# First six head pairs of an attention stage turned by TensorE in float32, low parts subtracted in one piece, and the planner's order made anew

## The chip, the cores and the metric

The kernel runs on one core of one Trainium2 chip. The metric is device time in microseconds (us) of that core, from repeated runs; one further execution was profiled, and its trace gives every duration below. TensorE is called PE in the rows (PEld is its weight load), VectorE DVE, ScalarE ACT, GpSimd POOL; SP is the engine whose queue issues most DMAs.

## What is computed

Three stages, one behind the other: attention with a threshold, a feed-forward layer, and a soft mixture of experts over 32 slots.

```python
scores = (1/8) * q @ k^T                         # 4 batches, 8 heads, 576 x 576, head width 64
scores = where(scores >= max(scores) - tau, scores, -1e9)
attn   = exp(scores - max(scores)); attn /= attn.sum(-1) + 1e-9
x = concat_heads(attn @ v)                       # 2304 tokens x 512

h = x @ w_in;  x = max(0.01*h, h) @ w_out        # 512 -> 2048 -> 512

logits = x @ phi                                 # 2304 x 32
d = softmax(logits, over tokens); slot = d^T @ x # 32 x 512
out_e  = relu(slot_e @ w1_e) @ w2_e              # 8 experts, 4 slots each
y = softmax(logits, over slots) @ out
```

Inputs are float32, but `w_in` and `w_out` reach the kernel as 64-bit floats that it takes apart itself.

## The kernel before

**Tiles.** The 2304 tokens are 18 tiles of 128. Tiles 4 and 13 straddle two batches (64 tokens of each). For each tile, `attention(t)` works through 8 heads in 4 pairs. `head` forms the scores S (128 x 576) on PE with q split into a high part `qh` and a low part `ql`; DVE takes the row minimum of the negated scores into `th` (L1028), ACT takes the exponential into `ae` (L1055), DVE applies the threshold and sums the row into `z` (L1062).

**From weights to X.** The product with v needs the weights transposed. `moved(t, pr, ...)` does it by DMA, which takes 2-byte data: each head's `ae` is cast to float16 `ah` (L1203), the remainder `ae - ah` is the low part (L1213 for 512 columns and L1229 for the last 64), and one DMA transpose on SP's queue (L1243) turns the 9 blocks of 128 columns into `aT`. PE then multiplies 14 blocks of `aT` with the float16 high and low parts of v (`vx`, L1250) into the PSUM tile X: high by high, high by low, low by high. For a straddling tile each block is split into two halves of 64 rows, so a head takes 28 products. A function `turned` that transposes `ae` on PE in float32 is in the code, but the option `CT=()` uses it for no tile.

**Feed.** X is divided by the row sums, transposed by PE (L1104) and split into float16 parts `xT`. `feed(t, xT)` multiplies with `wh`, the float16 parts of `w_in` (L1283, 48 products of 512 columns a tile), ACT applies the leaky rectifier into `r` (L1295), PE transposes `r` (L1316, copies in L1322 and L1324), and products with `wq` (L1335, four column groups of 32) give the logits. `wq` is `w_out` times `phi`, formed once: 16 chunks of `w_out` are converted, transposed by PE (L778), copied, and multiplied with phi (L794: four float32 products, the chunk's transpose as the stationary operand, 32 columns of phi moving). `block` (L1467 and its neighbours) joins two tiles into the running softmax over tokens.

**v.** `load_v(b)` loads v of a batch in four tiles `vr` of 10 x 64 columns, sums their absolute values on ACT (L957), and `split_v` scales them (L973), casts the high part (L983) and subtracts the low part (L988).

**Order.** Nothing here runs in the order of the code. Every operation is handed to a planner (`Plan`) with a priority, a planned duration and, where two engines can do it, alternatives. `schedule` simulates the five engines and the DMA queues with these planned durations, and the order that comes out is what each engine's queue holds. Each engine then works through its own queue in that order, and waits on semaphores where an operand or a buffer isn't ready. `O` holds the options: buffer counts (`VR` is the number of `vr` tiles), priorities, and planned costs. PSUM has 2 score tiles, 1 X tile and 3 tiles `h` that all other PE results share.

**Tail.** After the last tile, `w_out` (4 MB, from a copy `scr` in device memory), `w1` and `w2` (33 MB together) are loaded into whatever buffers are free (`CH`: `wh`, `kx`, `vr`, `vx`, `r`, ...), multiplied, and the result is stored.

## Time and profile before

| | |
|---|---|
| median of 3 runs | 682.22 us (680.89 to 683.32) |
| profiled execution, its own time | 679.31 us |
| its span, first to last instruction | 677.5 us |
| PE busy | 566.5 us (84%) |
| DVE / ACT / POOL busy | 454.3 / 440.2 / 289.9 us |
| mean granted clock of PE | 0.956 |
| DMA packets | 126.37 MB, mean 187 GB/s |

PE's matmul rows overlap each other, since matmuls are pipelined, so the busy time of one row says less than the distance between two rows. In the chain of work that ended last, rows of one kind are merged, and a row's length there is that distance. A granted clock of 1.00 is the 2.4 GHz level; a stretch whose mean is lower ran part of the time at 1.2 GHz.

### The profile page before, as it was taken

What the parts mean: (1) busy time and instruction counts of PE and PEld (TensorE: products, weight loads), DVE (VectorE), ACT (ScalarE), POOL (GpSimd) and SP (SyncE); (2) the same over time, 40 slices, a digit from 0 to 9 for tenths busy, and PEclk for the clock granted to TensorE, in tenths of its full rate; (3) what the DMA queues carried; (4) which work ended last, traced back from release to release, by engine and by line L of the source; (5) the groups of instructions that cost most, each with busy time, mean ns of one, the idle gap of its engine ahead of it and who ended that gap; (6) DMA issues with size and microseconds to landing.
All of it is one profiled execution on the core that took longest, in us unless ns stands there. A gap on an engine that the chain in (4) does not pass through costs nothing.

```text
span 677.5 us, 15209 instructions
## 1 busy us (share of the span) xinstructions
PE 566.5 (84%) x5640; PEld 380.8 (56%) x5640; DVE 454.3 (67%) x1112; ACT 440.2 (65%) x825; POOL 289.9 (43%) x339
## 2 busy tenths in 40 slices
PE   0101766998899999899999999979999999789995
PEld 0000655867567776665676776757667555333553
DVE  6989869786589789788798888767888300110023
ACT  7999768775467877688977787757777344320022
POOL 3565537351244755577854566646445100000000
PEclk9999978697999999999999999989999999879997
DMA  8961799894976789868986777687679702999996
GB/s 303 320 218 60 201 204 231 235 201 156 154 139 142 160 155 155 124 118 182 174 161 119 145 138 142 131 162 150 109 110 213 181 17 93 358 314 351 349 351 235
DMA packets 224073, 126.37 MB, mean 187 GB/s; under 512 B 175872, under 2 KB 196864, under 8 KB 224000
## 3 DMA queue, kind: packets, MB, share of 16 engines
q1 hardware_dynamic: 221264, 120.43, 75.0%
q10 hardware_dynamic: 2736, 4.98, 2.7%
q8 instruction: 44, 0.72, 0.5%
q14 instruction: 29, 0.24, 0.1%
HBM read 73.99 MB, written 8.91 MB: 122 GB/s over the span
## 4 chain that ended last, share of the span: by engine, by line
PE 62%; DMA 12%; DVE 5%; ACT 4%; issue 2%; POOL 2%; SPq 0%; DVEq 0%; POOLq 0%; ACTq 0%
PE h L1283 21%; DMA aT<-ah 12%; PE S L1017 10%; PE X L1250 8%; PE S L1601 5%; PE h L1316 4%; PE X L1672 3%; PE h L1467 2%; PE h L1335 2%; PE h L794 2%; DVE ae L1028 1%; DVE ae L1062 1%; PE h L778 1%; PE h L1558 1%; POOL kx L931 1%
## 5 line engine op out<-in xcount | busy, mean ns | idle before, releaser
L1283 PE MATMUL h<-wh,xT 128*128 128x512 f16 x864 | 213.8, 381 | 0.3 <-ACT c L1363 0.3
L1213 POOL TENSOR_TENSOR ah<-ae,ah 128x512 f16<-128x512 f32 x103 | 121.8, 1184 | 94.6 <-ACT ah L1203 48.5
L1028 DVE TENSOR_SCALAR_CACHE_REDUCE ae<-S,c 128x576 f32<-128x576 f32 x144 | 115.5, 811 | 36.4 <-PE S L1017 26.5
L1055 ACT ACTIVATE ae<-ae,th 128x576 f32<-128x576 f32 x144 | 109.3, 769 | 21.2 <-DVE ae L1028 20.4
L1062 DVE SCALAR_TENSOR_TENSOR ae<-S,th,ae 128x576 f32<-128x576 f32 x144 | 114.9, 810 | 9.2 <-ACT ae L1055 7.9
L1283 PEld LDWEIGHTS <-xT 128*128 128x128 f16 x864 | 76.8, 99 | 69.5 <-issue 2.4
L1017 PE MATMUL S<-kx,qh 128*128 128x288 f32 x320 | 108.7, 357 | 8.4 <-DVE ae L1062 4.8
L1250 PE MATMUL X<-vx,aT 128*128 128x64 f16 (+1 forms) x2240 | 91.3, 197 | 17.5 <-DMA aT<-ah 17.3
L1250 PEld LDWEIGHTS <-aT 128*128 128x128 f16 (+1 forms) x2240 | 80.0, 103 | 39.6 <-DMA aT<-ah 25.7
L1017 PE MATMUL S<-kx,ql 128*128 128x288 f32 x320 | 92.3, 305 | 10.1 <-DVE ql L893 10.1
L1203 ACT ACTIVATE ah<-ae 128x576 f16<-128x576 f32 x124 | 83.6, 677 | 21.3 <-DMA aT<-ah 11.5
L1229 POOL TENSOR_TENSOR ah<-ae,ah 128x64 f16<-128x64 f32 x127 | 53.4, 422 | 62.1 <-ACT ah L1203 52.9
L1017 PEld LDWEIGHTS S<-kx,qh 128*128 128x128 f32 x320 | 61.8, 193 | 21.1 <-issue 10.2
L1017 PEld LDWEIGHTS S<-kx,ql 128*128 128x128 f32 x320 | 62.0, 194 | 11.7 <-DVE ql L893 10.4
L1295 ACT ACTIVATE r<-h 128x512 f32<-128x512 f32 x72 | 42.5, 590 | 25.8 <-PE h L1283 25.6
L1322 ACT ACTIVATE rT<-h 128x512 f32<-128x512 f32 x57 | 33.7, 594 | 29.0 <-PE h L1316 28.8
L893 POOL TENSOR_TENSOR ql<-qr,qh 128x512 fp32r<-128x512 f32 x30 | 39.2, 1306 | 22.6 <-ACT qh L884 21.9
L931 POOL TENSOR_TENSOR kx<-kr,kx 64x576 fp32r<-64x576 f32 x26 | 38.6, 1486 | 21.3 <-ACT kx L924 16.8
L1316 PE MATMUL h<-c,r 128*128 128x128 f32 x288 | 45.4, 283 | 0.8 <-ACT r L1295 0.7
L1316 PEld LDWEIGHTS h<-c,r 128*128 128x128 f32 x288 | 34.6, 145 | 8.5 <-issue 2.1
L495 PE MATMUL h<-c,tmp 128*1 128x128 f32 x16 | 4.3, 364 | 41.3 <-DVE tmp L562 38.0
L1213 DVE TENSOR_TENSOR ah<-ae,ah 128x512 f16<-128x512 f32 x41 | 32.5, 794 | 7.4 <-ACT ah L1203 6.9
(286 smaller groups left out, 842.4 us busy)
## 6 DMA issues: line engine op xcount, KB each, us to landing
qr<-in_q SPq DMA_DIRECT2D x33, 256.0 KB, 3.1
wh<-in_w SPq DMA_DIRECT2D x32, 256.0 KB, 5.6
kx<-in_w SPq DMA_DIRECT2D x22, 256.0 KB, 5.7
vr<-in_v SPq DMA_DIRECT2D x16, 320.0 KB, 3.2
rT<-in_w_out SPq DMA_DIRECT2D x20, 256.0 KB, 3.7
kr<-in_k SPq DMA_DIRECT2D x16, 288.0 KB, 3.0
r<-in_w SPq DMA_DIRECT2D x18, 256.0 KB, 5.1
ae<-in_w_in SPq DMA_DIRECT2D x8, 512.0 KB, 5.3
```

Source lines behind the costliest of these rows:

```text
L931: f = lambda eng, kx=kx, h=h, l=l: lambda: eng.tensor_tensor(out=kx.ap[l], in0=kr.ap[h], in1=f32(kx.ap[h]), op=ALU.subtract)
L1017: pe.matmul(out=ps.ap[:rows, n, :HALF], lhsT=l.ap[:, hd % 4, :rows], rhs=kt.ap[:, n * HALF : (n + 1) * HALF], start=(j == 0), stop=(j == 1 ...
L1028: lambda: dve.tensor_scalar(out=ev(), in0=ps.ap[:, :, :HALF], scalar1=nt.ap[:, 0:1], scalar2=None, op0=ALU.subtract, op1=ALU.min, accum_ou ...
L1055: lambda: act.activation(out=ae.ap[:, hd % 2], in_=ae.ap[:, hd % 2], func=AF.Exp, bias=th.ap[:, 0:1], scale=-1.0),
L1062: lambda: dve.scalar_tensor_tensor(out=ev(), in0=ps.ap[:, :, :HALF], scalar=th.ap[:, 0:1], in1=ev(), op0=ALU.is_le, op1=ALU.mult, accum_ou ...
L1203: ("act", t_act(S) + 100, (lambda i: lambda: act.activation(out=ah.ap[:, i, i * S : i * S + S], in_=ae.ap[:, i], func=AF.Copy))(i)),
L1213: f = lambda eng: lambda: eng.tensor_tensor(out=w0(ah.ap), in0=src(ae.ap), in1=hi(ah.ap), op=ALU.subtract)
L1229: f = lambda eng, i=i, lo1=lo1: lambda: eng.tensor_tensor(out=lo1(ah.ap), in0=ae.ap[:, i, (1 - i) * LC : (1 - i) * LC + D], in1=ah.ap[:, i ...
L1250: pe.matmul(out=X.ap[r0:r1, (2 * pr + i) * D : (2 * pr + i + 1) * D], lhsT=aT.ap[:, 8 - c if i else c, r0:r1], rhs=vtiles[b, pr].ap[:, wv, ...
L1283: pe.matmul(out=hp.ap, lhsT=xT.ap[:, wx * 4 + k], rhs=wh[k][j].ap[:, ww], start=(n == 0), stop=(n == 11),)
L1295: (lambda j, hp: lambda: act.activation(out=r[j].ap, in_=hp.ap, func=AF.Prelu, alpha=0.01))(j, hp),
L1316: pe.transpose(tp.ap[:, c], r[j].ap[:, c * P : (c + 1) * P], ident.ap)
```

## The change

Six things change.

1. **Turned pairs.** The option `CN={0: 4, 1: 2}` sends all four pairs of tile 0 and the last two pairs of tile 1 through `turned`. It no longer scales `ae` first, it writes the transposes (L1177) into three buffers taken from the ring `r`, and its ten float32 products (L1198) now have the transposed weights as the stationary operand and v (64 columns) as the moving one, with X in the same layout as in `moved`.
2. **Low parts in one piece.** The subtraction of the low part runs over 576 columns at once (L1229 in the new file). That shifts the low columns by 64, so v is also stored shifted by 64 rows: `vr` grows from 10 to 18 x 64 columns, `vx` from 20 to 28. `VR` goes from 5 to 4.
3. **Tail of v.** The last 64 rows of v for turned pairs come as a tile of their own (`vz`, in an `xT` buffer).
4. **w_out times phi on column groups.** Phi (32 columns) is the stationary operand now, the chunk's transpose moves (L794, four groups of 32 rows). A copy `us` and one product with `e4` (L812) add the four groups and turn the result.
5. **Straddling tiles.** The two 64-row halves of a block now follow each other directly, block by block.
6. **Planned costs.** A DMA transpose is planned at 185 instead of 112 ns a block, scores at 560 instead of 520, so the whole order is made anew. X is normalised in one way for all tiles.

```diff
-        KR=2, VR=5, ET=1, RAW=1, CP=(3,), CT=(), PM=(), PR=1, AHN=2,
+        KR=2, VR=4, ET=1, RAW=1, CN={0: 4, 1: 2}, PM=(), PR=1, AHN=2,
...
-        op = pl.add(prio, one("sp", 112.0 * blocks, fn), r, w, after)
-        op.hold = (max(1225.0, 398.0 + 112.0 * blocks), 1300.0)
+        op = pl.add(prio, one("sp", O["BT"] * blocks, fn), r, w, after)
+        op.hold = (max(1225.0, 398.0 + O["BT"] * blocks), 1300.0)
...
+        up, us = tmp([P, P], F32, "h"), tmp([P, P], F32, "lts")
+
+        def f(wt=wt, up=up):
+            for k in range(4):
+                pe.matmul(
+                    out=up.ap[32 * k : 32 * k + 32], lhsT=phi.ap[:, k], rhs=wt.ap[:, k],
+                    start=True, stop=True, skip_group_check=True,
+                )
...
-                pe.matmul(out=wpp.ap, lhsT=wt.ap[:, k], rhs=phi.ap[:, k], start=(k == 0), stop=(k == 3))
...
+            (lambda us, wpp: lambda: pe.matmul(
+                out=wpp.ap, lhsT=us.ap, rhs=e4.ap, start=True, stop=True))(us, wpp),
...
-    turns = lambda t: O["CP"] if t in O["CT"] else ()
+    turns = lambda t: range(4 - O["CN"].get(t, 0), 4)
+
+    VC = 18
...
-                ("act", t_act(10 * D) + 90, lambda: act.activation(
+                ("act", t_act(VC * D) + 90, lambda: act.activation(
                     out=vr.ap, in_=vr.ap, func=AF.Copy, scale=sv.ap[:, 0:1])),
...
-        pe_op(prio, 520 * len(todo), f, r=[qh, ql] + kts, w=[ps])
+        pe_op(prio, O["TS"] * len(todo), f, r=[qh, ql] + kts, w=[ps])
...
         def f():
-            for r0, r1, b in regs:
-                v = vflat[b, pr].ap.rearrange("p (c d) -> p c d", d=D)
+            for i in range(2):
                 for c in range(5):
-                    for i in range(2):
+                    for r0, r1, b in regs:
+                        v = vflat[b, pr].ap.rearrange("p (c d) -> p c d", d=D)
                         pe.matmul(
-                            out=X.ap[64 * i : 64 * i + 64, pr * P + r0 : pr * P + r1],
-                            lhsT=v[:, 4 * i + c if c < 4 else 8 + i],
-                            rhs=eT.ap[:, 5 * i + c if c < 4 else 4, r0:r1],
-                            start=(pr == 0 and c == 0 and r0 == 0), stop=(c == 4),
+                            out=X.ap[r0:r1, (2 * pr + i) * D : (2 * pr + i + 1) * D],
+                            lhsT=(eTs[i].ap[:, c] if c < 4 else eTs[2].ap[:, 0])[:, r0:r1],
+                            rhs=v[:, 4 * i + c] if c < 4 else vtail[b].ap[:, pr, i],
+                            start=(pr == 0 and i == 0 and c == 0), stop=(c == 4),
                             skip_group_check=True,
                         )
...
+                return lambda: eng.tensor_tensor(
+                    out=ah.ap[:, i, (1 - i) * S : (2 - i) * S], in0=ae.ap[:, i],
+                    in1=ah.ap[:, i, i * S : i * S + S], op=ALU.subtract,
+                )
...
-                for r0, r1, b in regs:
-                    for n, (c, wv, cv) in enumerate(todo):
+                for n, (c, cv) in enumerate(todo[i]):
+                    for r0, r1, b in regs:
```

What the planner makes of it is seen in three places. The first is PE's queue where tile 0's first products with v stand. S are score products, w and h under L778 and L794 are a chunk of `w_out`, c_189 and c_252 are phi, c_75 is the identity. Before, the first product with X stands behind the scores of five heads and two chunks:

```order
L1017 MATMUL S<-kx,ql 128x288
L778 MATMUL h<-c_75,w 128x128 x4
L495 MATMUL h<-c_75,tmp 1x128
L794 MATMUL h<-c_189,w 128x32 x4
L519 MATMUL h<-tmp,c_84 128x1
L1017 MATMUL S<-kx,qh 128x288
L1017 MATMUL S<-kx,ql 128x288
L1017 MATMUL S<-kx,qh 128x288
L1017 MATMUL S<-kx,ql 128x288
L1250 LDWEIGHTS aT
L1250 MATMUL X<-vx,aT 128x64
```

The same place after the change (L1060 are the scores, r is the buffer that holds the transposed weights, xT the tail of v):

```order
L1060 MATMUL S<-kx,qh 128x288
L1060 MATMUL S<-kx,ql 128x288
L1177 MATMUL h<-c_75,ae 128x128 x5
L778 MATMUL h<-c_75,w 128x128 x4
L1198 MATMUL X<-vr,r 128x64 x4
L1198 MATMUL X<-xT,r 128x64
L1198 MATMUL X<-vr,r 128x64 x4
L1198 MATMUL X<-xT,r 128x64
L794 MATMUL h<-w,c_252 32x128 x4
L1060 MATMUL S<-kx,qh 128x288
L1060 MATMUL S<-kx,ql 128x288
```

The transposes and products of a pair stand between the scores of the next heads, with no DMA between them.

The second place is PE's queue at the first feed product (L1283 before, L1288 after). Before, it follows the eleventh head's products with v, behind the scores of 17 heads:

```order
L1250 LDWEIGHTS aT
L1250 MATMUL X<-vx,aT 128x64
L1283 LDWEIGHTS xT
L1283 MATMUL h<-wh,xT 128x512
L1283 LDWEIGHTS xT
```

After, it stands behind the scores of 11 heads; x_1070 is tile 0's normalised X, and L812 is the new small product of the `w_out` chunk:

```order
L778 MATMUL h<-c_75,w 128x128 x4
L794 MATMUL h<-w,c_252 32x128 x4
L1151 MATMUL h<-c_75,x_1070 128x128 x4
L812 MATMUL h<-c_86,lts 128x32
L778 MATMUL h<-c_75,w 128x128 x4
L1060 MATMUL S<-kx,qh 128x288
L1060 MATMUL S<-kx,ql 128x288
L1060 MATMUL S<-kx,qh 128x288
L1060 MATMUL S<-kx,ql 128x288
L794 MATMUL h<-w,c_252 32x128 x4
L1288 LDWEIGHTS xT
L1288 MATMUL h<-wh,xT 128x512
```

The feed of tile 0 has moved up by the scores of six heads, and one more `w_out` chunk (ten instead of nine) has come ahead of it.

The third place is SP's queue while `w_out` is loaded (rT and raw are its buffers, scr its copy in device memory). Before, transposes stand between the loads:

```order
L591 DMA rT<-in_w_out 128x512 x2
L876 DMA qr<-in_q 128x512
L769 DMA scr<-w 128x512
L1243 DMA_TRANSPOSE aT<-ah 128x9x128
L591 DMA rT<-in_w_out 128x512 x2
L1243 DMA_TRANSPOSE aT<-ah 128x9x128
L769 DMA scr<-w 128x512
L1243 DMA_TRANSPOSE aT<-ah 128x9x128 x2
L769 DMA scr<-w 128x512
L591 DMA rT<-in_w_out 128x512
```

After:

```order
L591 DMA rT<-in_w_out 128x512 x2
L896 DMA qr<-in_q 128x512
L769 DMA scr<-w 128x512
L591 DMA rT<-in_w_out 128x512 x3
L980 DMA vr<-in_v 128x1152
L769 DMA scr<-w 128x512
L896 DMA qr<-in_q 128x512
L591 DMA rT<-in_w_out 128x512
L591 DMA raw<-in_w_out 128x512
L769 DMA scr<-w 128x512
```

The first transpose on SP's queue now stands behind all but two of the loads of `w_out` in that queue.

## Rows read from the trace of the kernel before

**Rows 1.** Windows: stretch, length, busy PE, PEld, DVE, ACT, POOL, clock, DMA, GB/s.

```profile
51.00:68.00 17.00, 1.74 (x5) 0.87 (x5) 16.63 (x36) 16.47 (x35) 8.60 (x8) 1.00 0.19 58
68.00:85.00 17.00, 13.32 (x69) 11.24 (x69) 14.61 (x36) 12.36 (x27) 9.07 (x10) 0.90 0.77 202
85.00:102.00 17.00, 11.20 (x119) 10.09 (x118) 11.54 (x35) 12.09 (x26) 5.84 (x7) 0.80 1.09 208
102.00:136.00 34.00, 27.34 (x230) 23.52 (x231) 28.97 (x68) 26.55 (x57) 17.66 (x21) 0.75 0.95 232
136.00:170.00 34.00, 30.35 (x266) 23.58 (x264) 25.96 (x60) 22.19 (x46) 10.80 (x13) 0.90 0.71 181
170.00:204.00 34.00, 30.80 (x349) 20.43 (x348) 25.03 (x58) 17.94 (x34) 12.55 (x15) 1.00 0.83 145
204.00:240.00 36.00, 36.00 (x446) 26.72 (x443) 30.82 (x68) 29.88 (x54) 23.14 (x27) 1.00 0.78 150
...
540.00:560.00 20.00, 20.00 (x163) 11.53 (x161) 1.13 (x5) 8.62 (x21) 0.50 (x1) 1.00 0.10 34
...
580.00:620.00 40.00, 33.49 (x186) 12.33 (x185) 5.13 (x14) 8.36 (x18) 0.35 (x1) 0.83 1.01 348
```

**Rows 2.** Timeline of PE: first scores, first feed products, scores of head 28.

```profile
69.07 0.61 PE L1017 MATMUL S<-kx,ql 128*128 128x288 f32 x1 [10.11 <-DVE ql L893]
...
128.47 1.95 PE L1283 MATMUL h<-wh,xT 128*128 128x512 f16 x6
...
164.88 0.38 PE L1017 MATMUL S<-kx,qh 128*128 128x288 f32 x1
```

**Rows 3.** Chain that ended last, 110 to 170 and 400 to 430 us: start, length.

```profile
118.91 1.91 PE h L794 x8
123.54 1.52 PE X L1250 x28
132.48 0.81 PE h L794 x8
...
401.14 0.41 PE X L1250 x14
401.55 1.29 PE h L1283 x6
403.90 0.44 PE h L1316 x4
406.04 1.01 PE h L1335 x32
408.31 0.14 PE h L1352 x2
419.38 0.90 PE X L1250 x28
```

**Rows 4.** Groups: line, engine, operation, count, busy us, mean ns, idle before.

```profile
L1213 POOL TENSOR_TENSOR ah<-ae,ah 128x512 f16<-128x512 f32 x103 | 121.8, 1184 | 94.6 <-ACT ah L1203 48.5 <-issue 22.6 <-DVE ah L1205 8.2
L1229 POOL TENSOR_TENSOR ah<-ae,ah 128x64 f16<-128x64 f32 x127 | 53.4, 422 | 62.1 <-ACT ah L1203 52.9 <-DVE ah L1205 5.6 <-ACT c L799 1.8
L1213 DVE TENSOR_TENSOR ah<-ae,ah 128x512 f16<-128x512 f32 x41 | 32.5, 794 | 7.4 <-ACT ah L1203 6.9
L973 ACT ACTIVATE vr<-vr,c 128x640 f32<-128x640 f32 x15 | 11.9, 816 | 0.4 <-DVE c L530 0.4
L983 ACT ACTIVATE vx<-vr 128x640 f16<-128x640 f32 x15 | 10.9, 725 | 1.4 <-PE X L1250 1.4
```

**Rows 5.** Waits of PE between 420 and 540 us: total, times, longest.

```profile
PE X L1250 <- DMA aT<-ah: 6.1, 7, 3.2
```

**Rows 6.** Timeline of ACT: the last of five passes over the next batch's v.

```profile
67.65 0.74 ACT L957 ACTIVATE xT<-vr 128x640 bf16<-128x640 f32 x1
```

**Rows 7.** Loads issued on ACT's queue, by line 591: count, ns min/median/max.

```profile
L591 ACTq DMA_DIRECT2D rT<-in_w_out x6: 334/337/434, 94.5 to 142.0; - x6
```

**Rows 8.** Waits of SP's queue between 540 and 600 us.

```profile
SPq L1589 <- PE h L1283: 31.0, 10, 15.8
```

More of the change, by code (lines that the diff above doesn't have):

```diff
@@ L406, in psum_buf @@
         return pl.buf(("h",), shape, F32, "misc")
-    pl.early.update(("T", "xp", "misc", "gT"))
+    pl.early.update(("T", "xp", "misc", "gT", "eT"))
     pl.cap["h", "h"] = 2
@@ L789, in emit @@
         )
-        wpp = tmp([P, NS], F32, "h")
-        def f(wt=wt, wpp=wpp):
-            for k in range(4):
-                pe.matmul(out=wpp.ap, lhsT=wt.ap[:, k], rhs=phi.ap[:, k], start=(k == 0), stop=(k == 3))
-        pe_op(PQ, 850, f, r=[wt, phi], w=[wpp])
+        up, us = tmp([P, P], F32, "h"), tmp([P, P], F32, "lts")
[5 more added lines that the diff above has]
+                )
+        pe_op(PQ, 330, f, r=[wt, phi], w=[up, us])
+        add_alt(
+            PQ,
+            [
+                ("act", 210, (lambda up, us: lambda: act.activation(
+                    out=us.ap, in_=up.ap, func=AF.Copy))(up, us)),
+                ("dve", 220, (lambda up, us: lambda: dve.tensor_copy(out=us.ap, in_=up.ap))(up, us)),
+            ],
+            r=[up], w=[us],
+        )
+        wpp = tmp([P, NS], F32, "h")
+        pe_op(
+            PQ, 130,
+            (lambda us, wpp: lambda: pe.matmul(
+                out=wpp.ap, lhsT=us.ap, rhs=e4.ap, start=True, stop=True))(us, wpp),
+            r=[us, e4], w=[wpp],
+        )
         act_op(
@@ new lines, in attention @@
+        dve_op(
+            p, P2(100),
+            lambda: dve.scalar_tensor_tensor(
+                out=z1.ap, in0=z.ap, scalar=1e-9, in1=zfr.ap, op0=ALU.add, op1=ALU.mult),
+            r=[z, zfr], w=[z1],
+        )
+        dve_op(p, 200, lambda: dve.reciprocal(out=rz.ap, in_=z1.ap), r=[z1], w=[rz])
+        x32 = pl.buf("x32", [P, DM])
+        dve_op(
+            p, 74 + 1.19 * DM,
+            lambda: dve.tensor_tensor(
+                out=x32.ap.rearrange("p (h d) -> p h d", d=D), in0=X.ap.rearrange("p (h d) -> p h d", d=D),
+                in1=rz.ap.unsqueeze(2).to_broadcast([P, H, D]), op=ALU.mult,
+            ),
+            r=[X, rz], w=[x32],
+        )
@@ L1122, in recip, with f @@
+        xp = pl.buf(("h",), [P, 4, P], F32, "xp")
+        def f():
+            for k in range(4):
+                pe.transpose(xp.ap[:, k], x32.ap[:, k * P : (k + 1) * P], ident.ap)
+        pe_op(p, 440, f, r=[x32, ident], w=[xp, xT])
+        act_op(
+            p, 602, lambda: act.activation(out=xT.ap[:, :4], in_=xp.ap, func=AF.Copy), r=[xp], w=[(xT, 0)]
         )
         dve_op(
-            p, 153 + 6 * (h1 - h0),
-            lambda: dve.reciprocal(out=rz.ap[:, : h1 - h0], in_=z1.ap[:, : h1 - h0]), r=[z1], w=[rz],
-        )
@@ L1258, in moved @@
             pe_op(
-                p + 0.22, 29 * 14 * len(regs), f, r=[aT] + [vtiles[b, pr] for _, _, b in regs], w=[X],
+                p + 0.22, 29 * 14 + 60 * len(regs), f, r=[aT] + [vtiles[b, pr] for _, _, b in regs], w=[X],
             )
@@ L1743, in host @@
     ka = ka.reshape(B, 4, P, S)
-    vf = v[:, :, :512].reshape(B, 4, 2, 4, P, D).transpose(0, 1, 4, 2, 3, 5).reshape(B, 4, P, 8, D)
-    vl = v[:, :, 512:].reshape(B, 4, 2, D, D).transpose(0, 1, 3, 2, 4)
-    va = np.concatenate([vf, np.concatenate([vl, vl], axis=2)], axis=3)
+    va = np.zeros((B, 4, P, 20, D), np.float32)
+    for i in range(2):
+        x = v[:, i::2]
+        cols = lambda c, r0, r1, k0: va[:, :, r0:r1, c].__setitem__(
+            slice(None), x[:, :, k0 : k0 + r1 - r0])
+        for c in range(4):
+            cols(4 * i + c, 0, P, c * P)
+        if i:
+            rest = ((9, (448, 512)), (14, (512, 0)), (15, (64, 128)), (16, (192, 256)), (17, (320, 384)))
+        else:
+            rest = ((8, (512, 0)), (10, (64, 128)), (11, (192, 256)), (12, (320, 384)), (13, (448, 512)))
+        for c, (k0, k1) in rest:
+            cols(c, 0, 64, k0)
+            cols(c, 64, P, k1)
+        cols(18 + i, 64 * i, 64 * i + 64, 512)
     def bits(w):
```

182 lines of the change are left out of this document (71 added, 111 removed).

## The prediction

> **What bounds the kernel now.** I read the windows first [rows 1]. Until 68 us TensorE has almost nothing to do (1.74 of the last 17 us) while ACT is busy 16.47 and DVE 16.63 of 17: they convert `w_in`. The first scores start at 69 us [rows 2]. From 204 us on TensorE is busy without a gap (36.00 of 36 us, clock 1.00), and it stays close to that until attention is over; from 540 to 560 us it still works off feed products while DVE has 1.13 us of work and the DMA engines are 10% busy. Then loads take over (348 GB/s from 580 us). So there are three limits: elementwise engines up to 69 us, TensorE from about 204 us to the end of the feed, and the weight loads of the tail, which wait for TensorE: SP's queue stands 31.0 us behind the last feed products that free `wh` [rows 8]. What ends the feed earlier therefore moves the whole tail.
>
> Between 68 and 204 us neither limit holds. TensorE is busy 13.32 + 11.20 + 27.34 + 30.35 + 30.80 = 113 of 136 us, so 23 us are idle, and the granted clock is 0.90, 0.80, 0.75, 0.90 and 1.00 in the five windows, which takes another 1.7 + 3.4 + 8.5 + 3.4 = 17 us of full-speed time [rows 1]. These 40 us are what an order can win. DVE is the busiest other engine there (106 of 136 us), and feed products, which would fill TensorE, do not start before 128.5 us [rows 2].
>
> **The change part by part.** Work of TensorE, from the distances in the chain [rows 3]:
>
> - *Turned pairs.* Removed: twelve heads of 14 float16 products, 0.41 us a head, 4.9 us. Added: 6 x 9 transposes. L1316 is the same operation, four in 0.44, so 5.9 us. Added: 6 x 10 float32 products with a 128-wide stationary operand and 64 columns moving, which the trace does not have. The nearest row is L794 (same stationary shape, 32 columns): four products (eight records) in 0.81 us, so 0.20 each and 12.2 us. The row shows that the load of the stationary side sets the distance, since 32 columns alone can't take 0.2 us where 128 columns of a transpose take 0.11; so I take 0.20 for 64 columns too. The lower bound is a transpose's 0.11 (6.6 us), the upper one L794 at the low clock, 1.91 us for four, 0.48 each (28.7 us).
> - *w_out on column groups.* L794 at 0.81 becomes four products like those of L1335 (16 in 1.01 us, 0.25 for four) and one like L1352 (0.14): 0.42 saved, 6.7 us over 16 chunks at the full clock.
> - Sum: -4.9 + 5.9 + 12.2 - 6.7 = 6.5 us more work at the full clock. At the low clock (0.76 for a head from the pair at 123.54, 0.48 a product, twice the transposes, w_out 1.91 to about 0.85) it is -9.1 + 11.9 + 28.7 - 17 = about 14 us.
> - *Straddling tiles.* A head takes 28 products in 0.90 us, an ordinary one 14 in 0.41 [rows 3]. In the new order neighbours write different halves of X. L1335, whose neighbours write different column groups, still takes 1.01 us for 32 records, 0.032 each; 28 records at this distance are 0.88 us, so 16 heads gain 0.3 us, nothing. The Trainium skill weighs this otherwise: "TensorE: Matmul & The Clock Gate", Part 3, says that products on different column groups run at the same time, a few ns apart. By that rule, as an estimate, a straddling head would take half of its 0.90 and the two tiles would give 7 us; the record distance of L1335 speaks against the full effect.
> - *Low parts.* POOL's 1184 and 422 ns [rows 4] become one of about 1184 plus 64 columns. The slope between the two rows is 762 ns for 448 columns, so about 1290: 0.3 us less a head. POOL and DVE are off the path in the saturated stage, so it shortens only the way from scores to `aT`.
> - *v.* Scale and cast of a `vr` tile (816 and 725 ns at 640 columns [rows 4]) grow by 1.8 at most, 1.2 us a pair, 4.9 us for batch 0, on ACT, which is full before 69 us. Against that, before the change five passes over the next batch's v stand on ACT ahead of 69 us (the last at 67.65, 0.74 and a read of the sum each [rows 6]), about 4.5 us; with four `vr` tiles, all kept by the turned pairs, they move behind tile 1. Net zero. Batch 0 brings 1.6 MB more through DMA, 4.6 us at the 348 GB/s that the tail reaches; the last window before 68 us has room (0.19 [rows 1]), but these loads stand ahead of the last of `w_in`. I take +2 us for the start, bounds 0 and +5.
> - *Loads on ACT's queue.* The order moves 26 loads from SP to ACT for the rest of the run. One costs 0.34 us [rows 7], 9 us in all over 400 us in which ACT has slack (29.88 of 36 us at the fullest); nothing, unless one waits for its buffer at the head of ACT's queue, behind which the exponentials stand.
> - *Fewer vr tiles.* One tail load less can be fetched early: 256 KB, +0.7 us.
>
> **What the order gains** is read at one point. The scores of head 28 start at 164.88 us now [rows 2]. In the order, what DVE and ACT have ahead of head 28 is alike in both versions: all of `w_in`, all 16 chunks of `w_out`, 27 first and 26 second passes. DVE loses four casts and one of four low subtractions (0.8 us each [rows 4]) and gets six copies of transposed weights and eight of `us`; ACT loses nine casts and gets twelve copies. These cancel within 3 us. So head 28 should come at the same time, 165 us, plus the 2 us of the start. But TensorE has then issued more: 81 instead of 48 feed products (33 x 0.215 = 7.1), products with v of 22 instead of 16 heads (6 x 0.41 = 2.5), 24 instead of 16 transposes of `r` (0.9), 16 instead of none of L1335 (1.0), 8 instead of 4 transposes of x (0.4), and the last `w_out` product and one L1352 (0.9). That is 12.8 us less to do from there on, the 6.5 us of extra work already behind. From 165 us TensorE is nearly full in both, so this goes to the end.
>
> It needs about 19 us more work of TensorE in the same 96 us. At the clock of these windows the work of before (about 57 us at full speed, by the distances above) fills 68; 76 us would fill 91. With the gaps filled the clock should be higher: the stretch from 204 us, without gaps, shows 1.00 [rows 1]. I charge 2 us for gaps that stay.
>
> **Later waits.** Between 420 and 540 us TensorE waits 6.1 us for transposes [rows 5]. They are now planned at 185 ns a block, and the order puts slightly more of TensorE's work between a head's scores and its products with v (in the last 24 heads 11.8 instead of 10.6 us at the distances of [rows 3]). I take 2 of the 6.1 us, bounds 0 and 6.
>
> **Sum:** -12.8 + 2 (start) + 2 (gaps) - 2 (waits) + 0.7 (tail) = -10.1 us. The profiled execution took 679.3 us by its own clock, 1.8 more than its span, so 669.2; it lies 2.9 us under the median of the three runs, so the median should be 672.
>
> **Rivals.**
>
> - *A: forecast*, 672 us. Its own range is 663 to 679: start 0 to 5, gaps 0 to 6, waits 0 to 6, products at 0.11 (-5) or a little over 0.2.
> - *B: nothing is won*, 682 us. The 20 us of idle time between 68 and 170 us come from waits for DVE and ACT in a queue that is worked through in order; if each new transpose waits for its exponential as the transposes by DMA did, head 28 slips by what TensorE has gained. For it: DVE's share there. Against it: the waits are at score and chunk rows, and the new work stands between them.
> - *C: slower*, 690 us. The low clock stays: the float32 products cost 0.48 us and stand in TensorE's queue ahead of the next scores, so that attention itself is held. Work then fills 91 us at the old mean clock, and with the old 20 us of idle time head 28 comes 15 us later, which is 2.5 us more than the gain; extra work at the low clock instead of the full one adds another 7, for 10 in all, less the waits. It decides if the granted clock from 85 to 136 us stays at 0.80 or less.
> - *D: more is won*, 660 us: the gaps close fully and the clock is 1.00 from 100 us on, so that more than the 12.8 us is ahead at head 28, and the later waits go.
> - *E: straddling halves overlap*: if the halves of a block run side by side, 16 heads of 0.90 us [rows 3] take half, 7 us on top of A, 665 us. For it is L1335, whose neighbours write different column groups: 16 float32 products of 128 columns in 1.01 us are too fast for one after another (a transpose of 128 columns takes 0.11, a float32 product two records). Against it: 0.032 a record may already be the floor. (This is the rule of the page named above.)
>
> Chances: A 0.45, B 0.16, C 0.15, D 0.12, E 0.12. About 0.3%, 2 us, is what a measurement of this kernel can tell from no change. Faster by more than that: A, D, E and a little of B, less A's upper edge, 0.69; the same 0.11; slower 0.20. The range for 8 in 10 takes in D and E, and B with part of C: 657 to 688 us.
>
> **What the profile after would show.** Right: first feed products at about 115 us instead of 128.5; head 28 at 165 to 169 us with 81 feed products before it; granted clock above 0.85 from 102 to 136 us; ten turned products of a pair in about 2 us; the last feed products 10 us earlier and a tail of the old length. Wrong: first scores later than 74 us (the v loads or the longer passes cost more), turned products at 0.4 us and a clock that stays low (C), waits of TensorE for exponentials at the new transposes (B), or a new wait for `aT` behind tile 1, where the order now leaves 10 instead of 20 us between scores and products of tiles 2 and 3.

## The result and the profile after

The changed kernel takes 657.78 us (median of 4 runs, 653.94 to 660.11), beside 681.56 us for the kernel before (4 runs, 680.29 to 683.32). The ratio is 0.9644, 95% interval 0.9588 to 0.9699: faster, by 23.8 us where 10 were forecast. Runs on another chip gave 654.77 us (6 runs) beside 676.02, ratio 0.9674 (0.9622 to 0.9726). A time here and below is the median of all runs of a kernel, and a ratio counts only the runs within 1.5% of its fastest. The profiled execution took 656.39 us against 679.31, its span is 654.6 against 677.5 us, the mean granted clock 0.982 against 0.956.

The windows of the changed kernel answer to [rows 1]; columns as there:

```profile
68.00:85.00 17.00, 13.13 (x92) 11.12 (x92) 14.78 (x33) 11.23 (x28) 4.41 (x3) 1.00 0.69 200
85.00:102.00 17.00, 14.54 (x133) 12.52 (x134) 14.42 (x37) 14.86 (x41) 1.28 (x1) 1.00 0.83 286
102.00:136.00 34.00, 28.99 (x275) 20.69 (x274) 28.16 (x66) 26.90 (x63) 6.63 (x5) 1.00 0.78 185
136.00:170.00 34.00, 32.53 (x328) 24.64 (x327) 27.39 (x68) 25.12 (x50) 13.95 (x11) 1.00 0.80 198
170.00:204.00 34.00, 33.92 (x387) 23.44 (x386) 30.36 (x79) 29.63 (x48) 19.55 (x16) 1.00 0.80 167
204.00:240.00 36.00, 36.00 (x478) 24.91 (x476) 30.77 (x79) 27.93 (x53) 17.47 (x17) 1.00 0.78 170
```

From 68 to 204 us TensorE is busy 123.11 of 136 us, 10.1 more than before, and the granted clock is at the 2.4 GHz level in every window. The line to look at twice is 170 to 204: 33.92 us of TensorE where before had 30.80, and ACT at 29.63 where before had 17.94. I had called that stretch nearly full in both.

The timeline of TensorE answers to [rows 2]: first scores, the ten turned products of a pair, first feed products, the scores of head 28 and of head 29, the last feed products.

```profile
68.65 0.61 PE L1060 MATMUL S<-kx,ql 128*128 128x288 f32 x1 [1.50 <-DVE ql L913]
...
79.53 1.00 PE L1198 MATMUL X<-vr,r 128*128 128x64 f32 x8
80.37 0.39 PE L1198 MATMUL X<-xT,r 128*128 128x64 f32 x2
80.60 1.06 PE L1198 MATMUL X<-vr,r 128*128 128x64 f32 x8
81.49 0.39 PE L1198 MATMUL X<-xT,r 128*128 128x64 f32 x2
...
111.81 0.82 PE L1288 MATMUL h<-wh,xT 128*128 128x512 f16 x3
...
166.37 0.37 PE L1060 MATMUL S<-kx,qh 128*128 128x288 f32 x1
...
169.71 0.38 PE L1060 MATMUL S<-kx,qh 128*128 128x288 f32 x1
...
558.16 1.03 PE L1288 MATMUL h<-wh,xT 128*128 128x512 f16 x4
```

The turned products of a pair take 2.3 us (79.53 to 81.81, twenty records, 0.11 each), the first feed products come 16.7 us earlier than in [rows 2], head 28 only 1.5 us later. What I had not looked at is the next head. In the kernel before, the timeline of TensorE from head 28's last score on reads:

```profile
165.35 0.29 PE L1017 MATMUL S<-kx,ql 128*128 128x288 f32 x1
...
167.20 0.57 PE L1250 MATMUL X<-vx,aT 128*128 128x64 f16 x14
167.70 1.08 PE L1335 MATMUL h<-rT,c 128*32 128x128 f32 x32
168.71 0.99 PE L1250 MATMUL X<-vx,aT 128*128 128x64 f16 x28
...
175.29 0.58 PE L1250 MATMUL X<-vx,aT 128*128 128x64 f16 x14 [2.78 <-DMA aT<-ah]
...
180.69 0.58 PE L1250 MATMUL X<-vx,aT 128*128 128x64 f16 x14
...
182.11 0.38 PE L1017 MATMUL S<-kx,qh 128*128 128x288 f32 x1
```

There the order puts the products with v of seven heads (98 products) between head 28 and head 29, and TensorE's queue is worked through in order: no scores for 17 us. SP's queue of the kernel before shows why the last of these products came late, and the window what that cost the other engines:

```profile
154.38 0.33 SPq L876 DMA_DIRECT2D qr<-in_q  x1
156.47 0.33 SPq L769 DMA_DIRECT2D scr<-w  x1
157.62 0.33 SPq L1527 DMA_DIRECT2D raw<-scr  x1
158.69 5.71 SPq L769 DMA_DIRECT2D scr<-w  x2
164.50 2.79 SPq L1527 DMA_DIRECT2D w<-scr  x4
167.34 0.42 SPq L876 DMA_DIRECT2D qr<-in_q  x1
167.81 15.31 SPq L1243 DMA_TRANSPOSE aT<-ah  x7
```

```profile
160.00:182.00 22.00, 18.95 (x214) 13.95 (x214) 10.31 (x24) 8.51 (x18) 2.12 (x3) 0.92 0.79 164
```

Seven transposes stand back to back, 2.19 us each; the old plan counted 1.41 us for one. DVE and ACT, which live on scores, have 10.31 and 8.51 us of work in 22. The same window of the changed kernel:

```profile
160.00:182.00 22.00, 21.82 (x260) 16.10 (x258) 18.08 (x47) 18.33 (x34) 14.88 (x13) 1.00 0.83 149
```

At head 29 the changed kernel is 12.4 us ahead (169.71 against 182.11), and its order has 12 feed products and 4 transposes of `r` more behind it by then (12 x 0.215 + 0.4 = 3 us), with as many heads multiplied with v: 15 us of the 22.9. At head 28, 11.3 us of them were there already (the 12.8 us of work that the prediction counts, less the 1.5 us by which that head came later), so the place itself adds some 4 us. A second part lies in the straddling tiles. In the chain of the changed kernel a head of tile 13, 28 products in [rows 3] as well, reads:

```profile
406.47 0.56 PE X L1256 x28
411.26 0.56 PE X L1256 x28
```

0.56 us instead of 0.90, over 16 heads 5.4 us. In the single records, the two halves of a block start 0.003 us apart and the next block 0.032 us later, so that 28 products start within 0.44 us; in the kernel before neighbours stand 0.032 us apart, but where the halves change, and it takes 0.78 us. The 0.12 us from the last start to the next operation are the same in both. The last feed products start 21.9 us earlier than before (558.16 against 580.01), and what follows them is 1.0 us shorter.

### The profile page after: what moved, and what is told of

Same layout as the page of the kernel before. It is cut to its first block, busy times and chain, and to the rows that moved or that the text cites. A ratio compares the mean times of both kernels' runs of the same rounds, so it can differ in the third digit from the quotient of the medians.

```text
span 654.6 us, 15007 instructions
## 1 busy us (share of the span) xinstructions
PE 555.0 (85%) x5678; PEld 370.0 (57%) x5678; DVE 452.7 (69%) x1112; ACT 447.1 (68%) x823; POOL 249.4 (38%) x208
## 5 line engine op out<-in xcount | busy, mean ns | idle before, releaser
L1288 PE MATMUL h<-wh,xT 128*128 128x512 f16 x864 | 215.3, 381 | 1.0 <-DVE xT L1159 0.9
L1229 POOL TENSOR_TENSOR ah<-ae,ah 128x576 f16<-128x576 f32 x104 | 135.3, 1308 | 151.5 <-ACT ah L1218 101.0
L1060 PE MATMUL S<-kx,qh 128*128 128x288 f32 x320 | 107.9, 354 | 13.6 <-ACT qh L904 13.3
L1288 PEld LDWEIGHTS <-xT 128*128 128x128 f16 x864 | 76.8, 99 | 68.4 <-issue 1.5
L1060 PE MATMUL S<-kx,ql 128*128 128x288 f32 x320 | 90.3, 298 | 1.5 <-DVE ql L913 1.5
L1256 PE MATMUL X<-vx,aT 128*128 128x64 f16 (+1 forms) x2072 | 75.7, 194 | 13.3 <-DMA aT<-ah 13.1
L1256 PEld LDWEIGHTS <-aT 128*128 128x128 f16 (+1 forms) x2072 | 65.9, 101 | 33.9 <-DMA aT<-ah 17.1
L1218 ACT ACTIVATE ah<-ae 128x576 f16<-128x576 f32 x108 | 72.7, 678 | 15.0 <-DVE ae L1105 8.6
L1060 PEld LDWEIGHTS S<-kx,qh 128*128 128x128 f32 x320 | 60.0, 187 | 28.3 <-POOL kx L951 13.8
L1060 PEld LDWEIGHTS S<-kx,ql 128*128 128x128 f32 x320 | 60.1, 188 | 3.1 <-DVE ql L913 1.8
L1327 ACT ACTIVATE rT<-h 128x512 f32<-128x512 f32 x51 | 30.3, 595 | 26.1 <-PE h L1321 25.7
L951 POOL TENSOR_TENSOR kx<-kr,kx 64x576 fp32r<-64x576 f32 x21 | 31.1, 1482 | 20.2 <-DVE kx L946 10.0
L1363 DVE TENSOR_REDUCE sm<-h 128x1 f32<-128x32 f32 x18 | 3.4, 189 | 36.1 <-PE h L1357 35.9
L1229 DVE TENSOR_TENSOR ah<-ae,ah 128x576 f16<-128x576 f32 x28 | 22.3, 798 | 5.2 <-ACT ah L1218 5.0
```

What stands on the lines that cost most here:

```text
L1060: pe.matmul(out=ps.ap[:rows, n, :HALF], lhsT=l.ap[:, hd % 4, :rows], rhs=kt.ap[:, n * HALF : (n + 1) * HALF], start=(j == 0), stop=(j == 1 ...
L1218: ("act", t_act(S) + 100, (lambda i: lambda: act.activation(out=ah.ap[:, i, i * S : i * S + S], in_=ae.ap[:, i], func=AF.Copy))(i)),
L1229: return lambda: eng.tensor_tensor(out=ah.ap[:, i, (1 - i) * S : (2 - i) * S], in0=ae.ap[:, i], in1=ah.ap[:, i, i * S : i * S + S], op=ALU ...
L1256: pe.matmul(out=X.ap[r0:r1, (2 * pr + i) * D : (2 * pr + i + 1) * D], lhsT=aT.ap[:, c, r0:r1], rhs=vtiles[b, pr].ap[:, cv], start=(pr == 0 ...
L1288: pe.matmul(out=hp.ap, lhsT=xT.ap[:, wx * 4 + k], rhs=wh[k][j].ap[:, ww], start=(n == 0), stop=(n == 11),)
```

## The experiments

The theories, as they stood at the start: **Q**, the transposes by DMA stand in SP's queue behind the traffic of `w_out`, and turned pairs go round it; **K**, the gain is the clock, raised by the new product of `w_out` and phi; **P**, the planned costs carry it; **O**, neighbouring products on different halves of X overlap. The expectations use these letters. Unless the text says that the order is unchanged, the planner made a new one. Ratios are to the kernel before on the same chip, with 95% intervals.

### One part undone in the changed kernel

**No turned pairs.**

```diff
-CN={0: 4, 1: 2}
+CN={}
```

> The changed kernel without turned pairs: all pairs go through DMA transposes, all else as changed, the order planned anew. Theory Q (the transposes by DMA stand in SP's queue behind the stores and loads of w_out, and the turned pairs go round that queue): 8 to 12 us are lost, 666 to 670 us; the first feed product comes after 122 us, and TensorE again waits for aT and idles between 136 and 204 us. Rival K (the gain is the clock, raised by the new form of the product of w_out and phi): 658 to 661 us, and the granted clock from 68 to 204 us stays at 1.00.

662.34 us, ratio 0.9756 (0.9678 to 0.9835), so 5 to 8 us lost, by the two ratios of the changed kernel, with intervals that still overlap. The first feed products start at 130.91 us. The granted clock from 102 to 136 us is 0.74 and TensorE is busy 25.00 of 34 us there. K falls: the new product was in, and the clock was low all the same. Q's signs are there, its size of 8 to 12 us is not quite reached; the cause is taken up below.

**The old product of w_out and phi.**

```diff
-                pe.matmul(out=up.ap[32 * k : 32 * k + 32], lhsT=phi.ap[:, k], rhs=wt.ap[:, k], ...)
+                pe.matmul(out=wpp.ap, lhsT=wt.ap[:, k], rhs=phi.ap[:, k], start=(k == 0), stop=(k == 3))
```

> The changed kernel with the old product of w_out and phi (128-wide stationary operand, 32 columns moving), the order planned anew. Theory Q: only the longer product counts, 0.4 us a chunk at the full clock, and some of it in gaps: 660 to 666 us; the granted clock from 85 to 170 us stays above 0.93. Rival K: the clock falls back to 0.75 to 0.90 from 68 to 170 us, and 12 us or more are lost: 670 us or longer.

662.09 us, ratio 0.9707 (0.9615 to 0.9800): 2 to 4 us by the middle values, inside the intervals. The clock is 1.00, 1.00, 0.85 and 1.00 in the four windows from 68 to 170 us. K falls here too.

**The old planned costs.**

```diff
-TS=560, BT=185.0
+TS=520, BT=112.0
```

> The changed kernel planned with the old costs (112 ns a block for a DMA transpose, 520 for scores). Theory Q: the operations carry the gain and not the planned costs: 656 to 662 us. Rival P (the planned costs carry it, since the order then leaves the transposes by DMA their true time): 666 us or longer, with TensorE's waits for aT doubled from 204 us on.

672.13 us, ratio 0.9868 (0.9819 to 0.9918): 13 to 15 us lost, more than by any other part. P's size, though TensorE's waits for `aT` from 170 to 540 us are 9.9 us here and 9.5 in the changed kernel, not doubled: the loss is not in that row. Much of it lies earlier. From 102 to 136 us the clock is 0.77 here, and head 29 starts 5.7 us later than in the changed kernel, with 72 instead of 90 feed products behind it (18 x 0.215 = 3.9 us); between the two profiled executions there are 15.0 us. The timeline of TensorE at heads 28 and 29:

```profile
172.58 0.38 PE L1060 MATMUL S<-kx,qh 128*128 128x288 f32 x1
...
175.38 0.48 PE L1060 MATMUL S<-kx,qh 128*128 128x288 f32 x1
```

The place where the kernel before issued no scores for 17 us is not in this order, though it was made with the old costs.

**A cost moved by 4 ns**, to see what a new order alone does.

```diff
-TS=560
+TS=556
```

> The changed kernel with one planned cost moved by 4 ns (scores at 556 instead of 560), so that the order is made anew and nothing else differs. If an order made anew moves the time by itself only little, 656 to 660 us, and differences of 4 us and more between re-planned kernels can be read as those of their edits. If the order is a lottery, it comes 4 us or more away from 657.8 us, and single re-planned kernels say little.

657.97 us, ratio 0.9692 (0.9618 to 0.9766): the same as the changed kernel within the intervals.

**The changed kernel again, the old sequence in straddling tiles, and the low part in two pieces.** The last two keep the order as it is.

> The changed kernel once more, on the chip of the next runs, for their comparison: 656 to 660 us.

```diff
-                for n, (c, cv) in enumerate(todo[i]):
-                    for r0, r1, b in regs:
+                for r0, r1, b in regs:
+                    for n, (c, cv) in enumerate(todo[i]):
```

> The changed kernel, its order unchanged, with the products of a straddling tile in the old sequence (all of one half, then all of the other). Theory O (neighbouring products that write different halves of X overlap): 28 products take 0.90 us instead of 0.56, 16 heads, 5.4 us longer than the changed kernel, 662 to 664 us. Rival (the distance was shorter for another reason, such as the clock or better placed operands): no more than 1 us longer.

```diff
-                return lambda: eng.tensor_tensor(
-                    out=ah.ap[:, i, (1 - i) * S : (2 - i) * S], in0=ae.ap[:, i], ...)
+                    for c0, c1 in ((0, S - D), (S - D, S)):
+                        eng.tensor_tensor(
+                            out=ah.ap[:, i, (1 - i) * S + c0 : (1 - i) * S + c1], in0=ae.ap[:, i, c0:c1], ...)
```

> The changed kernel, its order unchanged, with the low part subtracted in two instructions again (512 and 64 columns). If the shorter way from scores to transpose carries part of the later stretch's gain, 0.3 us a head shows as more waits of TensorE for aT: 3 to 6 us longer than the changed kernel. If POOL and DVE are off the path there: within 1.5 us of it.

The changed kernel: 654.77 us, 0.9674, a little under the range expected. Old sequence: 661.05 us, 0.9749 (0.9693 to 0.9804), the chain's rows for the same heads at 0.90 us again:

```profile
408.24 0.90 PE X L1256 x28
413.36 0.90 PE X L1256 x28
```

With the order kept, the sequence alone decides between 0.56 and 0.90 us, as O says. The time, 5 to 6 us by the middle values, agrees with 16 x 0.34 = 5.4, with intervals that still overlap. A part is paid back in waits here too: TensorE waits for `aT` 6.2 us from 170 to 540 us with the old sequence, 9.5 and 7.2 in the two profiled executions of the changed kernel. Low part in two pieces: 663.51 us, 0.9802 (0.9751 to 0.9853), 8.7 us longer, more than the 3 to 6 expected. TensorE's waits from 170 to 540 us are, in this order,

```profile
PE X L1260 <- DMA aT<-ah: 13.9, 8, 3.8
```

where the changed kernel has

```profile
PE X L1256 <- DMA aT<-ah: 9.5, 6, 2.2
```

So 0.3 us on the way to each transpose is not free: 4.4 us come back as waits of TensorE alone (6.7 against the second execution of the changed kernel, which has 7.2).

### One part alone in the kernel before

**The straddling sequence, order unchanged.**

```diff
-                for r0, r1, b in regs:
-                    for n, (c, wv, cv) in enumerate(todo):
+                for n, (c, wv, cv) in enumerate(todo):
+                    for r0, r1, b in regs:
```

> The kernel before, its order unchanged, with the two halves of each block as neighbours (two loops exchanged, nothing else). Theory O: 28 products in 0.56 instead of 0.90 us, 16 heads: 5.4 us faster than before, 675 to 677 us, ratio 0.990 to 0.994. Rival (nothing overlaps, or the time is lost again in waits for aT): 681 to 682 us, ratio 0.997 or more.

677.34 us, ratio 1.0006 (0.9976 to 1.0036): nothing. The products do take 0.56 us, but the waits in its trace from 170 to 540 us, and those of the kernel before, are:

```profile
PE X L1250 <- DMA aT<-ah: 17.6, 17, 4.0
```

```profile
PE X L1250 <- DMA aT<-ah: 13.3, 15, 3.2
```

4.3 of the 5.4 us that TensorE saves it waits longer for the transposes. These are single executions; waits of one order differed by 2.3 us between two of them (above).

**SP's queue without the traffic of w_out, order otherwise unchanged.** The copy of `w_out` is left out: its stores are gone, and the loads that read it come later, from other data.

```diff
-                (lambda c, w: lambda dq: dq.dma_start(out=scr[c], in_=w.ap))(c, w),
+                lambda dq: None,
...
-            WO, t_dma(P * DM * 4), (lambda c, wo: lambda dq: dq.dma_start(out=wo.ap, in_=scr[c]))(c, wo),
+            WO, t_dma(P * DM * 4), late_load(c, wo),
```

> The kernel before without the 16 stores of w_out's copy on SP's queue, and with the loads of that copy behind attention (from other data of the same size); all other rows in their old order. It leaves out the copy of w_out. Theory Q (before, SP's queue of transposes stands behind stores that wait for w_out's conversion): the transposes that stood still from 148 to 168 us come earlier, and 5 to 9 us are won: 667 to 671 us where before takes 676, ratio 0.986 to 0.993. Rival P (the planned order decides, and a clear queue moves nothing since TensorE's own order waits): ratio 0.997 to 1.003.

684.36 us, ratio 1.0102 (1.0039 to 1.0165): slower by 1%. Q falls as it was put. Its queue at the same place:

```profile
150.32 1.64 SPq L591 DMA_DIRECT2D rT<-in_w_out  x2
154.41 10.58 SPq L876 DMA_DIRECT2D qr<-in_q  x2
165.43 8.15 SPq L1243 DMA_TRANSPOSE aT<-ah  x3
```

```profile
SPq L876 <- DVE ql L893: 9.8, 1, 9.8
```

With the stores gone, the transposes stand behind a load of q that waits 9.8 us for its buffer. They start 2.4 us earlier than before, and the products with v still stand in TensorE's queue ahead of the scores. With the order kept, the stores are not what costs the time. That turned pairs go round the queue in a new order is not refuted by this (see the two runs without them below).

**The two new planned costs.**

```diff
-        op = pl.add(prio, one("sp", 112.0 * blocks, fn), r, w, after)
-        op.hold = (max(1225.0, 398.0 + 112.0 * blocks), 1300.0)
+        op = pl.add(prio, one("sp", 185.0 * blocks, fn), r, w, after)
+        op.hold = (max(1225.0, 398.0 + 185.0 * blocks), 1300.0)
...
-        pe_op(prio, 520 * len(todo), f, r=[qh, ql] + kts, w=[ps])
+        pe_op(prio, 560 * len(todo), f, r=[qh, ql] + kts, w=[ps])
```

> The kernel before, planned with the new costs alone (185 ns a block for a DMA transpose, 560 for scores). Since the changed kernel lost 14 us with the old costs, theory P expects that the costs win by themselves: 8 to 14 us faster than before, 662 to 668 us, with the waits of TensorE for aT from 170 us on at half of their 13.3 us. Theory Q: within 3 us of before, since the queue behind w_out is as it was.

660.82 us, ratio 0.9762 (0.9702 to 0.9822), with not one operation changed: 16 us, more than the 8 to 14 that P expected. P is right. TensorE waits for `aT` 4.9 us from 170 to 540 us.

**Low part in one piece and straddling sequence, without and with the new costs** (the changed kernel with no turned pairs and the old product of `w_out`; the line of costs below for the first run alone).

```diff
-CN={0: 4, 1: 2}
+CN={}
-TS=560, BT=185.0
+TS=520, BT=112.0
```

> The changed kernel with three parts undone: no turned pairs, the old product of w_out and phi, the old planned costs. What is left of the change is the low part in one piece and the sequence of the straddling tiles. If these two carry 5 and 9 us by themselves (what undoing each cost in the changed kernel): 662 to 666 us where before takes 676, ratio 0.979 to 0.986. If they count only in an order that leaves TensorE no waits for aT (as for the straddling sequence in the kernel before): 672 us or longer, ratio 0.994 or more.

> As the run before it with the new planned costs: the low part in one piece, the sequence of the straddling tiles and the costs, but no turned pairs and the old product of w_out and phi. Theory P: 8 to 14 us faster than with the old costs, 655 to 664 us, so near the changed kernel. Theory Q: 5 us or more slower than the changed kernel, 661 us or longer, TensorE idle between 102 and 170 us and the first feed product after 122 us.

675.71 us (661.54 to 677.38), 0.9839 (0.9723 to 0.9955) from two of its six runs, so that the first stays undecided, and 668.41 us, 0.9860 (0.9803 to 0.9918). P's expectation fails for the second. Q's time holds, and TensorE idles 9.3 us from 102 to 170 us, but the first feed product comes at 119.16 us, not after 122. With the new costs and two parts that save work it is longer than the kernel before with the costs alone (0.9762). Parts don't add up over new orders; the longer passes over v and one `vr` tile less, which came with the low part, are in it too and weren't tried alone.

The second run holds two things more. It differs from the run with the old product (0.9707) in the turned pairs alone, and is 10 us longer, so here they carry what Q expected of them. And it has the bad place of the kernel before, though it was planned with 185 ns: eight transposes stand back to back behind the loads of `w_out`, and between heads 28 and 29 there are no scores for 16 us.

```profile
164.74 20.18 SPq L1230 DMA_TRANSPOSE aT<-ah  x8
```

```profile
159.68 0.44 PE L1041 MATMUL S<-kx,ql 128*128 128x288 f32 x1
...
164.13 1.39 PE L1237 MATMUL X<-vx,aT 128*128 128x64 f16 x42
...
171.26 0.58 PE L1237 MATMUL X<-vx,aT 128*128 128x64 f16 x14 [1.51 <-DMA aT<-ah]
...
176.11 0.48 PE L1041 MATMUL S<-kx,qh 128*128 128x288 f32 x1
```

**Which cost, and is it any new order?** The cost of a transpose alone, the cost of scores alone (the first and second half of the diff above), and a nudge of 4 ns; and the changed kernel with a transpose planned still longer.

```diff
-        pe_op(prio, 520 * len(todo), f, r=[qh, ql] + kts, w=[ps])
+        pe_op(prio, 516 * len(todo), f, r=[qh, ql] + kts, w=[ps])
...
-TS=560, BT=185.0
+TS=560, BT=215.0
```

> The kernel before, planned with 185 instead of 112 ns a block for a DMA transpose and nothing else. The trace of before shows a transpose every 2.2 us where they stand back to back; it was planned at 1.4 us (398 + 9 x 112 ns) and now is at 2.1. If this is what the two new costs win (16 us): ratio 0.972 to 0.982, TensorE's waits for aT from 170 us on down from 13.3 us to 5 or 6. If the scores' cost does it, or only both together: ratio 0.992 or more.

> The kernel before, planned with 560 instead of 520 ns for a block of scores and nothing else. If the transposes' cost carries the gain: ratio 0.995 to 1.005, with the waits for aT as before. If the scores' cost does it, since PE is then planned fuller: ratio 0.972 to 0.985.

> The kernel before with one planned cost moved by 4 ns (scores at 516 instead of 520): how much an order made anew moves the time of the kernel before. If its order is no bad draw: ratio 0.995 to 1.005. If any new order would have won, since this one is an unlucky one: ratio 0.985 or less.

> The changed kernel with a DMA transpose planned at 215 ns a block, 2.33 us in all, which is what 14 of them back to back take in its trace (32.86 us, 2.35 each). If a plan with true durations is what wins: 1 to 5 us faster than the changed kernel, ratio to before 0.960 to 0.966. If 185 already leaves enough room: the same as the changed kernel, 0.964 to 0.970.

The transposes' cost alone: 658.05 us, 0.9704 (0.9650 to 0.9758), 20 us. The scores' cost alone: 676.49 us, 0.9968 (0.9929 to 1.0007). The nudge: 674.35 us, 0.9942 (0.9907 to 0.9977). So in the kernel before it is this one number; the two other new orders won 2 and 4 us. It isn't mainly the waits for `aT`: from 170 to 540 us they fall from 13.3 to 8.6 us, not to the 5 or 6 expected. The window and the timeline of TensorE with the 185 ns, at the place where the kernel before stood:

```profile
160.00:182.00 22.00, 21.91 (x275) 17.26 (x275) 19.32 (x45) 15.20 (x29) 10.07 (x12) 1.00 0.84 182
```

```profile
163.65 0.38 PE L1017 MATMUL S<-kx,qh 128*128 128x288 f32 x1
...
164.26 0.58 PE L1250 MATMUL X<-vx,aT 128*128 128x64 f16 x14
164.68 0.81 PE L1283 MATMUL h<-wh,xT 128*128 128x512 f16 x3
165.42 1.08 PE L1335 MATMUL h<-rT,c 128*32 128x128 f32 x32
166.44 0.40 PE L1017 MATMUL S<-kx,qh 128*128 128x288 f32 x1
```

Head 29 starts at 166.44 us instead of 182.11, with the same 78 feed products behind it: the order now lays one head's products between two heads' scores instead of seven. That lead of 15.7 us compares with 17.7 between the two profiled executions. But about 12 us of it are older than this place: head 28 (163.65) has 75 feed products and 23 heads multiplied with v behind it, in the kernel before 48 and 16. The new order has spread that work over the time from 100 us on (SP's queue takes 18 transposes from 95 to 160 us, before 14). With 215 ns: 657.38 us, 0.9665 (0.9607 to 0.9723), the same as the changed kernel; 185 leaves enough room.

**Two last ones**: the 185 ns with the straddling sequence in the kernel before (the order that of the 185 ns alone), and the changed kernel with the old cost of scores and the new 185 ns, as a version that might beat both.

```diff
-TS=560, BT=185.0
+TS=520, BT=185.0
```

> The kernel before with two small edits: a DMA transpose planned at 185 ns a block, and the halves of a straddling tile's blocks as neighbours. In the kernel before that sequence won nothing, because TensorE's waits for aT grew by as much. If it counts once the order leaves room for the transposes: 3 to 5 us faster than with the 185 ns alone (ratio 0.9704), so 0.963 to 0.967, as good as the whole change. If it is lost in waits again: 0.970 or more.

> The changed kernel with the scores planned at 520 again and the DMA transposes at the new 185 ns a block: the one new cost without the other, in search of a version that beats both. If the cost of a transpose carries it all: 0.962 to 0.970, the same as the changed kernel. If the two costs belong together: 0.973 or more.

660.23 us, 0.9744 (0.9691 to 0.9796): no gain that can be measured over the 185 ns alone. In its profiled execution the last feed products do start 3.0 us earlier (560.63 against 563.63), so this one stays open. The second: 669.48 us, 0.9865 (0.9815 to 0.9914), 13 us longer than the changed kernel, as with both old costs. So in the changed kernel, with 185 ns, it is the scores' cost that matters, which did nothing in the kernel before, and with 520 the transposes' cost wins nothing (0.9868 and 0.9865). The scores' 560 with the old 112 ns was not run. By the scores the order made with 520 seems to keep pace until 350 us (TensorE's 384th recorded score product at 349.13 us, 348.70 in the changed kernel), but it has 396 instead of 411 feed products behind it there, 3.2 us of work, and at head 29 it was 5.3 us late with 9 feed products fewer. The rest goes by the 639th (516.19 against 501.83); from 400 to 540 us TensorE is busy 132.29 us, 136.02 in the changed kernel, and its two longest waits there are 4.0 us for a transpose and 1.7 for a part of k. Why the planner's order with 520 comes out so was not found.

## Why the prediction was wrong, point by point

The direction was right, the size was not: 672 us forecast, 657.8 measured, 24 us won instead of 10.

- **The step that failed**: "From 165 us TensorE is nearly full in both, so this goes to the end." I read the lead at head 28 alone, at 8.8 us net of start and gaps. It is 11.3 us there, and one head further 15: behind head 28 the order of before has its worst place, and what TensorE loses in it is not in the sum. Rows that I had read together, busy TensorE and granted clock, hid it: 18.95 of 22 us busy is nearly full, while the clock was 0.92, no scores were issued for 17 us and DVE stood at 10.31. With 5.4 us for the straddling tiles and 1.0 for the tail this is 21.4 of the 22.9 us between the two profiled executions. In the kernel before, the planned cost of a transpose alone takes the place away. But the place doesn't hang on that number: it stands in the run with the new costs and without turned pairs and new product, and not in the changed kernel with the old costs.
- **The planned costs** were priced at -2 us, by later waits for `aT`. They are the largest part from both sides: 16 to 20 us put into the kernel before, 13 to 15 us taken out of the changed one. I costed operations and let the order follow; here the order was the change.
- **"16 heads gain 0.3 us, nothing"** is refuted: 0.34 us a head, 5.4 in all (rival E's 7 was the right kind). I took the mean distance of the records of L1335, 0.032 us, for one between neighbours. In the trace of before these records come in fours, 0.007 us apart, with 0.109 us from four to four, so the row spoke for the overlap. The rule weighed in the prediction, of the Trainium skill's "TensorE: Matmul & The Clock Gate", Part 3, holds in this trace: products on different halves start 0.003 us apart. It is 38% and not half of the 0.90 us: the 0.12 us behind the last start stay, and where the halves change the old sequence had the same overlap. How much of the gain is left depends on the order: in that of before it turned into waits.
- **"Off the path in the saturated stage"**, of the low part, is refuted by the run with two pieces in an unchanged order: +8.7 us, of which 4.4 are seen as waits for `aT`.
- **Turned products** at 0.20 us: 2.3 us for ten, right. **The start**: +2 was forecast, the first scores came 0.4 us earlier; the 1.6 MB more for batch 0 are 1.3 by the sizes of the tiles (4 x 256 KB and 256 KB), and nothing hung on it. **Gaps and clock**: I had charged 2 us for gaps and expected above 0.85; 1.00 came in this execution, 0.70 to 0.90 in the repeated one between 85 and 136 us. **Later waits**: forecast shorter by 2 us; between 420 and 540 us they are 4.0 us now against 6.1 [rows 5], right. **Tail**: +0.7 forecast, shorter by about 1 us.
- **Rivals**: B is refuted by the time, C since the clock rose. D came nearest in time (660), for its waits and its clock in part, but at head 28 less than its 12.8 us was ahead. E was true beside it.

What stays open: how the 24 us divide among six edits, since every new order moves single kernels by some us and the parts don't add (the two runs without turned pairs and with the old product show it); whether the changed kernel is any faster than the kernel before with 185 ns alone (0.9644 and 0.9674 against 0.9704, intervals that overlap); by which of the planner's choices the costs work in the changed kernel, and whether the scores' cost would do it there without the transposes'. No version tried beats the changed one by more than the intervals; the one nearest to it is the kernel before with one number changed.

## What to carry to other kernels

Where a planner writes the order, check its durations against the trace first: an operation planned at 1.41 us that takes 2.19 in a burst went with an order that held scores behind seven heads' products, and mending that number alone won 20 us there. It is no rule: in the changed kernel with the old cost of scores the same number won nothing, so a planned cost has to be tried in the order at hand. When a lead is read at one point of two orders, read it also behind the next long wait, with the work that each order has done by then, and look at the starved engines (DVE at 10 of 22 us) instead of the busy share of the one that seems full. A saving on one engine counts only as far as the next one keeps up: 5.4 us of TensorE's work were worth about 5 by the middle values in one order and nothing in another.

## What the runs showed of the hardware

- Float16 products with 64 columns moving whose neighbours write different 64-row halves of one PSUM tile start 0.003 us apart, and the next two 0.032 us later (28 in 0.44 us from first to last start); neighbours that write the same half stand 0.032 apart (28 in 0.78, with the overlap once, where the halves change). Float32 products on four column groups of 32 start 0.007 us apart within a four, and 0.109 from four to four (before, from 405.97 us). Whether the products or the loads of their weights gain by it is not told apart.
- A float32 product with a 128-wide stationary operand takes 0.2 us in the chain of before with 32 columns moving (four in 0.81) and 0.22 to 0.23 with 64: doubling the columns changes little.
- The granted clock differs between runs of one kernel on one chip, and the time with it: six runs of the changed kernel lie between 650.28 us (0.990) and 659.03 us (0.967). Their mean is 0.981, that of the 17 runs of before on that chip 0.963; at the slope within each kernel (about 380 and 270 us for a clock of 1) that is, as an estimate, 5 to 7 of the 21 us between them there. Where in the run the clock falls differs as well: the two profiled executions of the changed kernel have 1.00 and 0.70 between 85 and 102 us.
